# Fused up-sampling attention and token/channel mixer on one core: one list scheduler orders the whole program

## The chip, the cores and the metric

The kernel runs on one core of a Trainium2 chip, as one launch for all eight batches. The metric is the device time of that core in microseconds. Five queues of instructions run beside each other: TensorE (PE, with its weight loads shown apart as PEld), VectorE (DVE), ScalarE (ACT), GpSimd (POOL) and SyncE (SP). Each works its own queue strictly in order; a row that waits holds all rows behind it. DMAs are issued from these queues, here mostly from SP and some from ACT.

## The reference, cut to what matters

```python
q_d, k_d, v_d = (t.reshape(B, H, S // 4, 4, D).mean(axis=3) for t in (q, k, v))
out_up = repeat(softmax(q_d @ k_d.T / sqrt(D)) @ v_d, 4, axis=2)
out_local = softmax(where(abs(pos_i - pos_j) < 4, q @ k.T / sqrt(D), -1e9)) @ v
x = (out_up + out_local), heads side by side      # (B, S, H*D)
h = maximum(x.T @ w_tok1, 0) @ w_tok2
u = x + h.T
out = u + maximum(u @ w_ch1, 0) @ w_ch2
```

There are B = 8 batches, H = 8 heads, S = 576 positions and D = 64; d_model is 512, the hidden sizes are 256 (tokens) and 1536 (channels). All is float32.

## The kernel before

A float32 matrix product is made of three float16 passes (`mm3`, line 124): each operand is split in an upper half and a rest, and the upper halves, and each upper half with the other's rest, are multiplied. So each operand costs an ACT instruction (the upper half) and a DVE instruction (the rest).

A batch `b` passes through these pieces; each is a Python generator that yields `step(engine, us, needs, take, give)` (line 150) before it emits an instruction or a group.

- `load_v` (455) loads eight tiles `vr` of values from SP (`fetch`, 461), squares each on ACT into `dump`, whose accumulator gives `vm` (486), and adds rows pairwise on POOL into `vd` (492, 493). From batch 2 on the tiles carry the tag `w`.
- `pool_q` (506), `pooled` (535) and `local` (592) are the two attentions: scores `sd`, exponentials `pd`, transposes `td` and `ptd`, product `ad` and result `od` for the pooled one; `pooled` ends with ACT issuing the copies of `od` into `vw` (587). The local one has windows of 38 columns, transposes `pT` and `pt`, and the product `av`, from which `x` comes.
- `mix` (666) is the token product: `splits` (675) of `x`, `products` (688) into `t`, `hid` and `t2`, `takes` (715) for `u` and its maximum `umx`, then `scaled` (748) for batches 0 and 1, which makes `uh`, or `mixtures` (766) for later batches. That one makes the four mixtures `s1`, `s2`, `s4`, `s3` of the quarters `a11` to `a22` of `u` on POOL (776), scales all seven to float16 upper halves on ACT (787) and takes their rests on DVE.
- The channel product of batches 0 and 1 is `first` (857, PE rows `c1`, `c<-uh,CW` in the profile) with `first_up` (877). Batches 2 to 7 use `product7` (887): for each of six pairs `p` of weight tiles seven block products with 288 columns instead of eight, in the PSUM banks `P`, `R` and `Q`. ACT copies three of them out (910: `x1`, `m5`, `u2`), DVE adds (955 and others), ACT takes four relus into `h` (918), DVE the rests.
- The block products need sums of weights. `weight_sums` (985) computes them once, on DVE and POOL during batch 1, and stores them in `sums`; `product7` loads three at a time as `t123`.
- `second` (1014, PE rows `c2`, `c<-h,CX` in the profile) and `second_up` (1029) make the second channel product, add it to `u` and store `out` (1039) from SP.

What sets the order: inside `tc.manual_schedule()` the function `drive` (170) is a list scheduler. It holds a clock for each engine in estimated microseconds, and among the next steps of all streams whose needs are made it takes the one that can start first; those of one engine within `PATIENCE` (0.15) of it compete by their rank in the table `ORDER`. In this kernel `drive` orders batch 0 and the beginning of batch 1, until the last `over` of batch 0 and `uh` of batch 1 are made, and returns the streams that are left over.

The rest is driven by hand: a `Run` (1121) steps the channel products of batch `b` in turn with their followers, and `tick` (1142) advances the side work, the attention and the token product of batch `b + 1` (`side`, 846), in proportion to the matmuls issued; `SIDE` = 42 and `FR` = 0.9 are the proportions, and `together` (806) steps up to `LIVE` + 1 streams of it by turns. Outside `manual_schedule` the framework orders instructions itself by priority; `tc.high_priority` and `tc.keep_in_program_order` steer that.

Buffers of the tags `w`, `m`, `g` and `gg` are chosen by `slot` (66). Under `drive`, a step that takes a slot (`take`) sets the number; otherwise `slot` counts up itself:

```python
    def slot(k):

        if not driven[0]:
            now_in[k] = (now_in[k] + 1) % SLOTS[k]
        return k + str(now_in[k])
```

The steps of `load_v` take no slot, and the loads of batch 2 stand within the part that `drive` orders.

Of the kernel before, what the change touches and what calls it, by code (L numbers as in the profile page):

```python
# [6 lines left out]
F32 = mybir.dt.float32  # L7
# [20 lines left out]
FR = 0.9  # L28
LIVE = 3
# [4 lines left out]
ORDER = ("T0 D1 A0 A7 D9 m0 D8 W2 W4 U0 M0 a7 N3 D10 M1 C2 M3 m1 M2 U1 W1 A6 A4 C11 W0 N1 A3 L2 D11 W3 A1 P0 "  # L34
         "C3 m3 D7 A8 S0 m2 H0 P1 C4 C0 L0 D5 D0 D4 a8 A5 L5 L1 h0 a0 Q0 L3 D3 C1 L4 a2 a6 C5 W6 N2 C6 D6 U2 "
         "C10 W7 C9 C8 a1 D2 N0 C7 W5 A2 a3 a4 W8 a5 ").split()
# [7 lines left out]
def tile_ups_attention_mixer(ctx, tc, qk, vw, vr, w1, w2, c1, c2, out):  # L44
# [125 lines left out]
    def drive(streams, until):  # L170

        items = [[g, next(g, None), 0.0, -ORDER.index(name)] for name, g in streams]
        driven[0] = True
        while not all(u in made for u in until):
            some = []
            for it in items:
                if it[1] is None or not may(it[1]):
# [23 lines left out]
            it[2] = t + us + 0.3  # L201
# [3 lines left out]
            try:  # L205
                it[1] = it[0].send(it[2])
            except StopIteration:
                it[1] = None
        driven[0] = False
        for k, n in SLOTS.items():  # L210
            first = min(free[k], key=free[k].get) if free[k] else [i for (x, _), v in held.items() for i in v if x.split(">")[0] == k][0]
            now_in[k] = (first - 1) % n
        return [it for it in items if it[1] is not None]

# [240 lines left out]
    def load_v(st):  # L455
# [18 lines left out]
        early = {0: 8, 1: 5}.get(st.b, 2)  # L474
        for i in range(early):
            yield step("S", ISSUE, *([("mixed", 0)] if st.b == 1 and i == 0 else []))
            fetch(i)
        for i in range(8):
# [3 lines left out]
            if st.b > 1 and i + 2 < 8:  # L482
                fetch(i + 2)
            t = ts.pop(i)
            e = yield step("A", 0.7, at=arrives[i])
            square = nc.scalar.activation(dump, t.rearrange("p r c -> p (r c)"), AF.Square, scale=2.0 ** -20,  # L486
                                          accum_out=st.vm[:, i:i + 1])
            if st.b > 1 and not driven[0]:
                tc.keep_in_program_order(square)
            make(("vm", st.b, i), e)  # L490
            e = yield step("G", 1.25)
# [43 lines left out]
    def pooled(st, pr):  # L535
# [41 lines left out]
        e = yield step("V", 0.65, give=one)  # L577
# [88 lines left out]
    def mix(st):  # L666
# [48 lines left out]
        def takes():  # L715
# [12 lines left out]
            for ch, two in WALK[b > 1]:  # L728
                s0, N = CHUNKS[ch]
                for c in (2 * two, 2 * two + 1):  # L730
                    yield step("A", 0.4, ("t2", b, ch, c), give=f"gg>{b}" if c % 2 else "")
                    if ch == 0:
                        st.u[c] = T([128, S], F32, "ts" if b == 1 and c > 1 else "u", f"u{b}_{c}")
# [491 lines left out]
```

## Time and profile before

| | us |
|---|---|
| runs, median (lowest to highest of three) | 954.78 (953.64 to 956.38) |
| the profiled execution | 949.53 |
| its span, first to last instruction | 947.8 |
| PE busy | 887.2 |
| PE weight loads busy | 659.0 |
| DVE busy | 529.5 |
| ACT busy | 423.6 |
| POOL busy | 297.2 |

The second part of the page cuts the span in 40 slices of 23.7 us; a digit is the busy share in tenths, 9 for 90% and more, and for `PEclk` the granted clock of TensorE in tenths.

```profile
PE   7787899996999989999999999999998999999998
ACT  4764673424432365344643355344653355332620
POOL 5998740412039730064005320054004230002000
PEclk9879999997999999999999999999999999999999
```

Two places show a granted clock under 9: slices 3 and 4 in the start, where weights are prepared, and slice 10, the passage from batch 0 to batch 1. Where a row of the trace has square brackets, they hold the time for which the engine stood idle ahead of it, and what ended that.

### The profile page before, as it was taken

Reading aid. Unit: us, or ns where it says so; the run is one execution under the profiler, and the core shown is the slowest. Engines: PE = TensorE matmul, PEld = TensorE weight load, DVE = VectorE, ACT = ScalarE, POOL = GpSimd, SP = SyncE. Lnnn points to the kernel's source line nnn. Section 1 sums busy time; section 2 is a strip of 40 time slices with the busy share of each in tenths; the row PEclk is TensorE's granted clock in tenths of the full one; section 3 lists DMA queues with packets and bytes.
Section 4 is the critical chain, followed back from the end, with each engine's and each line's share of the span. In section 5 each row is a group of like instructions: output and inputs, shape, how many; then the busy total and the mean of one; then the engine's idle time right before and its main releaser. Section 6 shows DMA issues by size and latency. Waiting matters only on the chain.

```text
span 947.8 us, 26409 instructions
## 1 busy us (share of the span) xinstructions
PE 887.2 (94%) x11218; PEld 659.0 (70%) x11218; DVE 529.5 (56%) x1287; ACT 423.6 (45%) x1004; POOL 297.2 (31%) x457
## 2 busy tenths in 40 slices
PE   7787899996999989999999999999998999999998
PEld 3544678664866758767776778767785768767776
DVE  7888877323667567534755267524754267433631
ACT  4764673424432365344643355344653355332620
POOL 5998740412039730064005320054004230002000
PEclk9879999997999999999999999999999999999999
DMA  9694330511034322340125102350126111100200
GB/s 262 185 297 132 117 81 26 180 34 39 21 136 104 107 64 71 103 157 28 55 90 180 47 30 71 121 140 32 53 89 181 42 35 52 54 21 19 74 20 33
DMA packets 35142, 84.87 MB, mean 90 GB/s; under 512 B 4272, under 2 KB 15536, under 8 KB 33776
## 3 DMA queue, kind: packets, MB, share of 16 engines
q1 hardware_dynamic: 32464, 80.82, 27.9%
q10 hardware_dynamic: 2560, 2.36, 0.9%
q8 instruction: 88, 1.44, 0.6%
q14 instruction: 30, 0.25, 0.1%
HBM read 69.01 MB, written 11.80 MB: 85 GB/s over the span
## 4 chain that ended last, share of the span: by engine, by line
PE 75%; DVE 14%; DMA 4%; ACT 3%; issue 3%; POOL 1%; ACTq 0%; POOLq 0%; DVEq 0%
PE c L124 31%; PE t L124 10%; PE P L124 9%; PE R L124 5%; PE ad L572 3%; PE av L641 3%; PE Q L124 2%; DMA vr<-in_vr_dram 2%; PE t L707 2%; PE sc L605 2%; PE pT L628 2%; PE td L563 2%; DMA vw<-od 1%; PE busy L168 1%; PE sd L544 1%
## 5 line engine op out<-in xcount | busy, mean ns | idle before, releaser
L124 PE MATMUL c<-h,CX 128*128 128x320 f16 (+1 forms) x2304 | 307.3, 286 | 1.3 <-issue 1.3
L124 PEld LDWEIGHTS <-CX 128*128 128x128 f16 x2304 | 222.2, 98 | 66.8 <-issue 5.3
L124 PEld LDWEIGHTS <-CW 128*128 128x128 f16 x1440 | 137.2, 99 | 52.3 <-issue 16.1
L1038 DVE SCALAR_TENSOR_TENSOR u<-c,io,u 128x256 f32<-128x256 f32 (+1 forms) x64 | 32.8, 513 | 103.8 <-PE c L124 103.6
L124 PE MATMUL c<-uh,CW 128*128 128x256 f16 (+1 forms) x576 | 80.7, 293 | 7.2 <-ACT uh L760 6.1
L518 POOL TENSOR_TENSOR qs<-qk 128x288 f32<-128x288 f32 x56 | 43.9, 784 | 137.8 <-DMA qk<-in_qk_dram 134.2
L492 POOL TENSOR_TENSOR vr<-vr 72x256 f32<-72x256 f32 x64 | 47.7, 745 | 113.2 <-ACT dump L486 112.5
L736 DVE TENSOR_REDUCE umx<-u 128x1 f32<-128x256 f32 (+1 forms) x64 | 28.3, 451 | 96.2 <-ACT u L734 96.1
L734 ACT ACTIVATE u<-t,down 128x256 f32<-128x256 f32 (+1 forms) x64 | 30.9, 495 | 102.9 <-PE t L124 102.9
L124 PEld LDWEIGHTS <-t 128*128 128x128 f16 x648 | 61.8, 98 | 18.6 <-issue 2.8
L124 PE MATMUL t<-xh,W 128*128 128x512 f16 (+1 forms) x240 | 61.2, 391 | 4.4 <-DVE xh L685 3.2
L124 PE MATMUL t<-W,hid 128*128 128x256 f16 (+1 forms) x384 | 58.8, 289 | 0.1
L458 POOL MEMSET vd<- 72x16 f32 x8 | 1.0, 123 | 161.9 <-PE ad L572 161.9
L685 DVE SCALAR_TENSOR_TENSOR xh<-x,back,xh 128x512 f16<-128x512 f32 (+1 forms) x40 | 34.0, 849 | 29.3 <-ACT xh L683 29.3
L486 ACT ACTIVATE dump<-vr 72x512 uint8<-72x512 f32 x64 | 39.7, 620 | 15.6 <-DMA vr<-in_vr_dram 15.5
L776 POOL TENSOR_TENSOR s<-u,u 128x288 f32<-128x288 f32 x12 | 9.3, 794 | 115.9 <-ACT u L734 115.9
L572 PE MATMUL ad<-vd,ptd 72*72 72x65 f32 x512 | 40.7, 232 | 3.8 <-issue 2.3
L556 ACT ACTIVATE pd<-sd,nmd 72x144 f32<-72x144 f32 x128 | 39.4, 373 | 9.8 <-DVE nmd L551 8.6
L124 PEld LDWEIGHTS <-W 128*128 128x128 f16 (+1 forms) x240 | 22.6, 99 | 29.4 <-issue 9.8
L572 PEld LDWEIGHTS ad<-vd,ptd 72*72 72x72 f32 x512 | 38.8, 149 | 5.9 <-issue 3.1
L641 PE MATMUL av<-vw,pt 47*32 47x64 f32 x2304 | 36.0, 234 | 6.4 <-issue 3.4
L124 PEld LDWEIGHTS <-hid 128*128 128x128 f16 x384 | 35.1, 98 | 9.5 <-ACT hid L721 0.4
(182 smaller groups left out, 1609.4 us busy)
## 6 DMA issues: line engine op xcount, KB each, us to landing
qk<-in_qk_dram SPq DMA_DIRECT2D x32, 579.0 KB
t<-sums SPq DMA_DIRECT2D x36, 384.0 KB
vw<-in_vw_dram SPq DMA_DIRECT2D x32, 351.0 KB
vr<-in_vr_dram SPq DMA_DIRECT2D x64, 144.0 KB
C_raw<-in_c_dram SPq DMA_DIRECT2D x16, 512.0 KB
out_dram<-u SPq DMA_DIRECT2D x32, 160.0 KB
C_raws<-in_c_dram SPq DMA_DIRECT2D x8, 512.0 KB
out_dram<-u SPq DMA_DIRECT2D x32, 128.0 KB
```

What stands on the lines that cost most here:

```text
L124: nc.tensor.matmul(ps, lhs(a), rhs(c), start=first and i == 0, stop=last and i == 2, **kw)
L486: square = nc.scalar.activation(dump, t.rearrange("p r c -> p (r c)"), AF.Square, scale=2.0 ** -20, accum_out=st.vm[:, i:i + 1])
L492: nc.gpsimd.tensor_add(t[:, 0:2], t[:, 0:2], t[:, 2:4])
L518: nc.gpsimd.tensor_add(two, x[:, :, 0:2], x[:, :, 2:4])
L556: nc.scalar.activation(pd[:, par, g], s[:, par, g], AF.Exp, bias=nm[:, par, g:g + 1], scale=0.125 / 16)
L563: nc.tensor.transpose(ps[:G, par, o:o + G], pd[:, par, g, G * kg:G * kg + G], ident[:G, :G])
L572: nc.tensor.matmul(ps[:, g, par], pt[:, par, kg, G * g:G * g + G], st.vd[:, kg, 2 * pr + par], start=kg == 0, stop=kg == 1)
L641: nc.tensor.matmul(ps[QB * j:QB * j + QB, par, D * hp:D * hp + D], pt[p, hp, QB * j:QB * j + QB], st.vw[h][p, g, D * hp:D * hp + D], start ...
L685: nc.vector.scalar_tensor_tensor(st.xh[t][:, 1], xf(t), back[:n], st.xh[t][:, 0], ALU.mult, ALU.subtract)
L734: nc.scalar.activation(st.u[c][:, s0:s0 + N], banks[ch, c // 2][:, c % 2, :N], AF.Copy, scale=st.down)
L736: nc.vector.tensor_reduce(st.umx[:, ch, c:c + 1], st.u[c][:, s0:s0 + N], axis=AX.X, op=ALU.max, apply_absolute_value=True)
L1038: nc.vector.scalar_tensor_tensor(u, banks[c, ch], io[:, ch:ch + 1], u, ALU.mult, ALU.add)
```

## The change

`drive` takes no `until` any more and runs until every stream has ended; it orders all eight batches inside `manual_schedule`, and `Run`, `tick`, `rest`, `together`, `attention`, `side`, `SIDE` as a number, `FR` and `LIVE` are gone. Every piece of the later batches is a stream with a rank in `ORDER`, and the dependences that were program order become `needs`.

The arithmetic stays. DVE, ACT and POOL have as many instructions as before (1290, 975 and 463 in the order listings); PE has four more matmuls of the filling `busy`, and SP six more stores of weight sums (18 instead of 12).

The scheduler, with the table of ranks:

```diff
-FR = 0.9
-LIVE = 3
...
+SIDE = "h b4 b5 b6 b7 b8 b0 b1 b2 b3 b9 n0 n2 n1 n3 n4 n5"
+SLACK = 0.8
...
+ORDER = ("u0 u1 u2".split() + [f"e{b}.{i}" for b in range(2, 8) for i in (0, 1, 2, 3, 4, 6, 5)] + ORDER
+         + [x[0] + str(b) + "." + x[1:] if x[1:] else x + str(b) for b in range(2, 8) for x in SIDE.split()]
+         + "p0 p1 p2".split() + [f"e{b}.7" for b in range(2, 8)])
...
-    def drive(streams, until):
-
-        items = [[g, next(g, None), 0.0, -ORDER.index(name)] for name, g in streams]
+    def drive(streams):
...
-        while not all(u in made for u in until):
+        while items:
...
-                t = max([clock[e], it[2] if at is None else at] + [made[n] for n in needs]
-                        + [min(free[k.split('>')[0]].values()) for k in take])
+                steady = ("uh", 1, 0) in made
+                t = max([0.0 if steady and at is None and it[4] == e else it[2] if at is None else at]
+                        + [made[n] for n in needs] + [min(free[k.split('>')[0]].values()) for k in take])
+                t = max(clock[e], t + (SLACK if e == "P" and steady else 0.0))
```

So a step of a stream whose last step was on the same engine needs no longer wait for its estimated end once `uh` of batch 1 is made, and a PE step is estimated to start 0.8 us after its last need.

The loads of `vr` take a slot of the tag `w` now, and give it back after the additions on POOL:

```diff
+        held_w = "w>v" if st.b > 1 else ""
         for i in range(early):
-            yield step("S", ISSUE, *([("mixed", 0)] if st.b == 1 and i == 0 else []))
+            yield step("S", ISSUE, *([("mixed", 0)] if st.b == 1 and i == 0 else []), take=held_w)
...
             if st.b > 1 and i + 2 < 8:
+                yield step("S", ISSUE, take=held_w)
...
-            e = yield step("G", 1.25)
+            e = yield step("G", 1.25, give=held_w)
```

`product7` is split in six streams: `copies`, `adds`, `relus`, `rests`, `fetch` (the loads of `t123`) and `products`; every step that used to be in one line of code has a need of its own. The first block product `s1` of a batch needs the whole of `c2` of the batch before, the first `a11` doesn't. Of the new functions the two on which the path runs:

```diff
+        def copies():
+            before = {("x1", 0): ("uh", b, "s2"), ("m5", 0): ("uh", b, "s2"), ("u2", 0): ("uh", b, "s4"),
+                      ("x1", 1): ("uh", b, "s4"), ("m5", 1): ("uh", b, "s3"), ("u2", 1): ("uh", b, "s3")}
+            for p in range(NP):
+                for n, x, r in (("x1", "a11", "P"), ("m5", "s1", "R"), ("u2", "s2", "P")):
+                    e = yield step("A", 0.4, ("p7", b, p, x), before[n, p] if p < 2 else ("rest", b, p - 2, n))
+                    plain[p, n] = T([128, HS], F32, "tm", f"{n}_{b}_{p}")
+                    nc.scalar.copy(plain[p, n], bank[p, r][:, :HS])
+                    make(("plain", b, p, n), e)
...
+                for x, w, r, first, last, needs in (
+                        ("a11", old(fa, 0), "P", True, False, None),
+                        ("s1", new(p, 0), "R", True, False, [("t123", b, p)]),
+                        ("s2", new(p, 1), "P", False, False, [("plain", b, p, "x1")]),
+                        ("a12", old(fa, 1), "Q", True, True, []),
+                        ("s4", old(fb, 1), "R", False, True, [("plain", b, p, "m5")]),
+                        ("s3", new(p, 2), "P", False, False, [("plain", b, p, "u2")]),
+                        ("a11", old(fa + 2, 0), "P", True, False, []),
+                        ("a22", old(fb, 0), "P", False, True, [("add", b, p, "m5")])):
...
+                    if x == "s1":
+                        needs += [("c2", b - 1)]
+                    e = yield step("P", us, ("uh", b, x), *needs, take=f"m>{r}{b}" if first else "")
+                    if first:
```

`mix` has six streams for batches from 2 on: `mixtures` (POOL), `upper` (the conversions on ACT) and `lower` (DVE) stand apart. `t2` of batch `b` needs the output of batch `b - 2` to be over, the final `od` of a batch needs the block products' inputs `("full", b - 1)`, and the local product `av` needs `("mixed", b - 1)`. Buffers of `u` in batch 1 are swapped: tiles 0 and 1 lie in the tag `ts`, which `t123` uses later, instead of 2 and 3. `weight_sums` is two streams, the additions on DVE and `weight_parts` (splits on POOL, three stores for each pair).

```diff
+        for b in range(2, B):
+            streams.append((f"h{b}", lazily(lambda b=b: ahead(b), *after(b - 1))))
+            some = attend(b) + [lazily(lambda b=b: value_scale(ready[b]), *(("vm", b, i) for i in range(8)))]
+            streams += [(f"b{b}.{i}", x) for i, x in enumerate(some)]
+            streams += [(f"n{b}.{i}", lazily(lambda b=b, i=i: mix_of(b)[i], ("q", b, 0))) for i in range(6)]
+            streams += [(f"e{b}.{i}", lazily(lambda b=b, i=i: channel_of(b, i), ("q", b, 3))) for i in range(8)]
+        drive(streams)
```

Three places show how rows move. The first is SP's queue at the end of batch 0 and the beginning of batch 1, with the semaphores for which each row waits: the loads of `vr` of batch 2 (`vr2_i`) and a store of `u0`. Before:

```order
L471 DMA vr2_0_2967<-in_vr_dram 72x512 [waits DMAHW7_49,Activation_49]
L1039 DMA out_0_dram<-u0_2_1284 128x320 [waits DMAHW0_49,DVE_49]
L471 DMA vr2_1_2983<-in_vr_dram 72x512 [waits DMAHW1_49,DMAHW7_49,Activation_49,Pool_49]
L471 DMA vr2_2_2985<-in_vr_dram 72x512 [waits DMAHW1_49,DMAHW2_49,Activation_49,Pool_49]
L471 DMA vr2_3_3023<-in_vr_dram 72x512 [waits DMAHW2_49,DMAHW3_49,Activation_49,Pool_49]
L471 DMA vr2_4_3044<-in_vr_dram 72x512 [waits DMAHW3_49,DMAHW4_49,Activation_49,Pool_49]
```

and in the change:

```order
L471 DMA vr2_0_2967<-in_vr_dram 72x512 [waits DMAHW7_49,Activation_49]
L471 DMA vr2_1_2970<-in_vr_dram 72x512 [waits DMAHW0_49,Activation_49]
L1025 DMA out_0_dram<-u0_2_1282 128x320 [waits DMAHW1_49,DVE_49]
L471 DMA vr2_2_2983<-in_vr_dram 72x512 [waits DMAHW2_49,Activation_49]
L471 DMA vr2_3_3026<-in_vr_dram 72x512 [waits DMAHW3_49,DMAHW7_49,Activation_49,Pool_49]
L471 DMA vr2_4_3057<-in_vr_dram 72x512 [waits DMAHW0_49,DMAHW4_49,Activation_49,Pool_49]
```

Before, every load from the second on waits for POOL, and for the transfer ahead of it; in the change the first three wait for no POOL row, and `vr2_3` is the first that does.

The second place is ACT's queue at the head of batch 3: `u3_c` are the tiles of `u`, `dump` the squares of the `vr` tiles of batch 4, `L619`, `pd4` and `ptd4` attention of batch 4, `a11h3` the first operand of batch 3's block products. Before:

```order
L734 ACTIVATE u3_2_6272<-t2_3_0_2_6174,down3_4959 128x256
L486 ACTIVATE dump_128,vm4_5965<-vr4_7_6172 72x512
L734 ACTIVATE u3_3_6278<-t2_3_0_2_6174,down3_4959 128x256
L734 ACTIVATE u3_2_6272<-t2_3_1_2_6209,down3_4959 128x320
L734 ACTIVATE u3_3_6278<-t2_3_1_2_6209,down3_4959 128x320
L787 ACTIVATE a11h3_6314<-u3_0_6092,us3_0_6298 128x288
```

and in the change:

```order
L734 ACTIVATE u3_3_6173<-t2_3_0_2_6042,down3_5486 128x256
L488 ACTIVATE dump_128,vm4_6059<-vr4_1_6102 72x512
L734 ACTIVATE u3_2_6089<-t2_3_1_2_6163,down3_5486 128x320
L734 ACTIVATE u3_3_6173<-t2_3_1_2_6163,down3_5486 128x320
L488 ACTIVATE dump_128,vm4_6059<-vr4_2_6118 72x512
L619 ACTIVATE P2_112<-P2_112 128x8x38
L488 ACTIVATE dump_128,vm4_6059<-vr4_3_6175 72x512
L619 ACTIVATE P0_110<-P0_110 128x8x38
L619 ACTIVATE P1_111<-P1_111 128x8x38
L566 COPY ptd4_0_6404<-td4_0_6373 72x576
L488 ACTIVATE dump_128,vm4_6059<-vr4_4_6238 72x512
L799 ACTIVATE a11h3_6458<-u3_0_6016,us3_0_6413 128x288
```

One square stood among the last four takes of `u` before; now four stand there and ahead of `a11h3`, with four rows of attention, and a fifth, that of `vr4_0`, in the row just ahead of these.

The third is ACT's queue at the fifth pair of block products of batch 3: `x13`, `m53` and `u23` (in the change `x1_3`, `m5_3`, `u2_3`) are the copies out of PSUM, `h3_4` the relus, and the DMAs from `od4` to `vw4` those of the pooled result of batch 4. Before:

```order
L918 ACTIVATE h3_4_6858<-u23_4_6899 128x288
L587 DMA vw4_0_5884<-od4_6544 8x9x256
L910 COPY x13_4_6944<-P_3_4_6937 128x288
L910 COPY m53_5_6971<-R_3_5_6964 128x288
L918 ACTIVATE h3_4_6858<-m53_4_6866 128x288
L918 ACTIVATE h3_4_6858<-P_3_3_6829 128x288
L632 COPY pt4_0_6963<-pT4_0_6958 128x512
L910 COPY u23_5_6980<-P_3_4_6937 128x288
L587 DMA vw4_0_5884<-od4_6544 8x9x256
```

and in the change:

```order
L922 COPY u2_3_4_7060<-P_3_4_7001 128x288
L587 DMA vw4_0_5886<-od4_6709 8x9x256 x2
L587 DMA vw4_1_5889<-od4_6709 8x9x256 x2
L940 ACTIVATE h3_4_7032<-x1_3_4_7017 128x288
L940 ACTIVATE h3_4_7032<-u2_3_4_7060 128x288
L940 ACTIVATE h3_4_7032<-m5_3_4_7048 128x288
L922 COPY x1_3_5_7105<-P_3_5_7095 128x288
L940 ACTIVATE h3_4_7032<-P_3_4_7001 128x288
L922 COPY m5_3_5_7130<-R_3_5_7114 128x288
```

Before, the first two of the four DMAs stood apart with six rows between them, and the other two later; now all four stand in one row (two rows of x2), ahead of the next relus and copies.

On PE the head of a batch changes too. Before, `second` of a batch ended, and then `a11`, two rows of `sd`, `s1` and `s2` of the next came, six matmuls for each block product. In the change the `a11` of batch 3 (6 matmuls) is followed by 36 matmuls of `c2` of batch 2, and only then by `s1`; `sd4_0` stands in the middle of `second` of batch 2.

More of the change, by code (lines that the diff above doesn't have):

```diff
@@ L207, in drive @@
             except StopIteration:
-                it[1] = None
+                items.remove(it)
         driven[0] = False
[L210 to L213, printed above, removed]
     count = [0]
@@ L764, in scaled @@
                 make(("uh", b, ch), e)
[L766 to L779 removed]
+        ORDER7 = ("a11", "s1", "s2", "a12", "s4", "s3", "a22")
@@ L801, in mixtures @@
-            yield from block("a22", A[1][1])
-            make(("uh", b), now[0])
-        return [splits(), products(), takes(), mixtures() if b > 1 else scaled()]
-    def together(todo, most):
-        live = []
-        while todo or live:
-            while todo and len(live) < most:
-                g = todo.pop(0)
-                live.append([g, next(g)])
-            some = False
-            for x in list(live):
-                if may(x[1]):
-                    some = True
-                    yield x[1]
-                    x[1] = next(x[0], None)
-                    if x[1] is None:
-                        live.remove(x)
-            if not some:
-                yield live[0][1]
@@ L824, in attention @@
-    def attention(st):
-        todo = [pooled(st, pr) for pr in range(4)] + [local(st, t) for t in range(len(TILES))]
-        yield from together([value_scale(st)] + todo, LIVE + 1)
+            make(("uh", b), now[0])
+        return [splits(), products(), takes()] + ([mixtures(), upper(), lower()] if b > 1 else [scaled()])
     def pool_all(st):
@@ L981, in product7 @@
-        make(("h", b), now[0])
-    sums = []
+                    make(("rest", b, p, n), e)
+                make(("hp", b, p), e)
+            make(("h", b), e)
+        return [copies(), adds(), relus(), rests(), fetch(), products()]
+    sums, parts7 = [], {}
     def weight_sums():
-        gates = [("c1", 1, 1, 3), ("c1", 1, 1, 7), ("c1", 1, 1, 11), ("c2", 1, 0, 0), ("c2", 1, 1, 0), ("c2", 1, 0, 1)]
         for p in range(NF // 2):
@@ L1067, in attend, with after @@
                 + [lazily(lambda t=t: local(ready[b], t), ok) for t in range(len(TILES))])
+    def after(b):
+        return [("x", b, t) for t in range(len(TILES))] + [("od", b, i) for i in range(4)]
     mixes = {}
@@ L1103, in tile_ups_attention_mixer @@
         group["Q"] = products[2:]
-        group["h"] = [lazily(lambda: ahead(2), ("x", 1, last))]
-        streams = [(f"{k}{i}", x) for k in "LMCTWUDSANmPHaQh" for i, x in enumerate(group[k])]
-        left = drive(streams, [("over", 0, 3)] + [("uh", 1, 0)] * (B > 1))
-    def rest(items):
-        while items:
-            some = False
-            for it in list(items):
-                if it[1] is None:
-                    items.remove(it)
-                elif may(it[1]):
-                    some = True
-                    yield it[1]
-                    it[1] = next(it[0], None)
-            if items and not some:
-                yield items[0][1]
@@ L1175, in tile_ups_attention_mixer, with late, channel_of @@
-    while work.next is not None:
-        work.go()
+        group["p"], group["u"], group["s"] = [], [], [lazily(f, ("c1", 1, 1, 1)) for f in (weight_sums, weight_parts)]
+        def late(what):
+            yield step("S", 0.0, ("q", 1, 3))
+            if not group["p"]:
+                group["u"], group["p"] = main(ready[1], (["h"] * 4, ["h"] * 4))
+            yield from what()
+        channel = {}
+        def channel_of(b, i):
+            if b not in channel:
+                st, banks = ready[b], {}
+                channel[b] = product7(st) + [second_up(st, banks), second(st, banks)]
+            return channel[b][i]
```

314 lines of the change are left out of this document (123 added, 191 removed).

## The prediction

> **What bounds the kernel now.** I read the head of the page first, to see which engine sets the time.
>
> ```profile
> span 947.8 us, 26409 instructions
> PE 887.2 (94%) x11218; PEld 659.0 (70%) x11218; DVE 529.5 (56%) x1287; ACT 423.6 (45%) x1004; POOL 297.2 (31%) x457
> ```
>
> TensorE is busy for 94% of the span and no other engine for more than 56%, so a reordering can win little more than the 60 us in which PE stands still, and what the throttle takes. Both programs hold the same arithmetic. The next view therefore asks where PE stands: the busy time by stretch, cut at the start of each stage (start and filling; products of batch 0; the passage to batch 1; batch 1; one stretch per batch 2 to 6, from its first block product to that of the next; batch 7). Columns: stretch, length, busy time and count of each engine, granted PE clock, DMA.
>
> ```profile
> core 0: us, PE busy (x) PEld busy (x) DVE busy (x) ACT busy (x) POOL busy (x), PEclk, DMA share, GB/s
> 0.00:102.20 102.20, 78.08 (x1020) 46.53 (x1020) 85.32 (x181) 60.83 (x128) 83.30 (x109) 0.87 0.70 213
> 102.20:205.00 102.80, 101.56 (x1369) 78.36 (x1368) 63.12 (x151) 50.93 (x113) 33.40 (x53) 1.00 0.30 88
> 205.00:240.00 35.00, 25.18 (x178) 17.35 (x177) 12.69 (x36) 14.28 (x41) 9.54 (x16) 0.80 0.12 35
> 240.00:342.10 102.10, 97.22 (x1299) 73.01 (x1297) 63.60 (x149) 33.64 (x79) 54.62 (x91) 1.00 0.31 96
> 342.10:447.75 105.65, 104.08 (x1353) 77.93 (x1353) 55.73 (x142) 50.56 (x125) 27.47 (x47) 0.98 0.27 84
> 447.75:554.07 106.32, 102.62 (x1366) 77.98 (x1364) 55.20 (x143) 48.91 (x122) 26.58 (x45) 1.00 0.27 85
> 554.07:661.76 107.69, 104.03 (x1378) 78.68 (x1375) 57.40 (x148) 51.43 (x128) 29.00 (x47) 1.00 0.28 84
> 661.76:769.82 108.06, 103.95 (x1361) 78.52 (x1362) 53.84 (x141) 47.59 (x118) 24.76 (x44) 0.98 0.28 84
> 769.82:875.87 106.05, 103.52 (x1370) 78.15 (x1368) 55.26 (x143) 45.01 (x108) 6.79 (x9) 1.00 0.12 38
> 875.87:947.80 71.93, 67.01 (x542) 52.52 (x539) 27.35 (x62) 20.39 (x51) 1.71 (x2) 1.00 0.13 42
> ```
>
> Length minus PE busy is PE's idle time: 24.1 us in the start, where DVE and POOL are busy over 80% of the time, 1.2 in batch 0, 9.8 in the passage, 4.9 in batch 1, then 1.6, 3.7, 3.7, 4.1 and 2.5 in the five middle stretches (15.6 together), and 4.9 in the last. The passage is the one sick place: 35 us of which PE works 25.2, at 0.80 of its clock, so at most 20.1 us of work; 14.9 us are lost. The timeline of the passage says why (start, length, engine, line, operation, in brackets the idle time before it and its releaser).
>
> ```profile
> 205.98 27.84 SPq L471 DMA_DIRECT2D vr<-in_vr_dram  x7
> 212.95 0.63 ACT L486 ACTIVATE dump<-vr 72x512 uint8<-72x512 f32 x1 [1.91 <-DMA vr<-in_vr_dram]
> 213.49 0.19 ACT L486 ACTIVATION_READ_ACCUMULATOR dump<-vr 72x1 f32 x1
> 214.60 0.51 POOL L493 TENSOR_TENSOR vd<-vr 72x128 f32<-72x128 f32 x1
> 217.55 0.63 ACT L486 ACTIVATE dump<-vr 72x512 uint8<-72x512 f32 x1 [3.47 <-DMA vr<-in_vr_dram]
> 218.17 0.51 ACT L734 ACTIVATE u<-t,down 128x320 f32<-128x320 f32 x1
> 226.83 0.63 ACT L486 ACTIVATE dump<-vr 72x512 uint8<-72x512 f32 x1 [1.29 <-DMA vr<-in_vr_dram]
> 227.46 0.49 ACT L760 ACTIVATE uh<-u,us 128x256 f16<-128x256 f32 x1
> 228.01 0.59 PE L124 MATMUL c<-uh,CW 128*128 128x256 f16 x2 [3.98 <-ACT uh L760]
> ```
>
> Seven loads of `vr` go out over 27.8 us, one every 4.6 us (212.95 to 217.55): each waits until the tile before it has been squared on ACT and added on POOL. The squares stand in ACT's row ahead of `u` and `uh` of batch 1, so ACT waits for the load, and PE waits 3.98 us for `uh`. The loads go one at a time because all of them sit in one buffer.
>
> **The change, part by part.** (A) The passage. The order listing of SP shows the loads in three buffers: only the fourth waits for POOL. The same loop of 4.6 us then delivers a tile every 1.5 us, and the five that are left after the first three take 7.7 us, beside products that PE has anyway. Of 14.9 us lost I take 13.5 as won. Bounds: 8, if ACT still waits for two of them, and 14.9.
>
> (B) Batch 1, 240 to 342 us: `t2` of batch 2, its maximum and the mixtures of `u` stood at the end, behind the last product; now 132 matmuls of `c2` of batch 1 and first scores of batch 3 stand between the last `t2` and the first block product, and weight sums are done by a stream of their own. POOL is busy 54.6 of these 102 us, so it has room. Idle is 4.9; I take 3.5, between 0 and 4.9.
>
> (C) The heads of batches 2 to 6. Where PE waits there, before:
>
> ```profile
> 454.15 0.77 PE L124 MATMUL P<-a11h,CW 128*128 128x288 f16 x5 [0.74 <-DVE x L955]
> 455.69 0.69 PE L563 MATMUL td<-ident,pd 72*72 72x72 f32 x8 [0.77 <-ACT pd L556]
> 661.76 0.91 PE L124 MATMUL P<-a11h,CW 128*128 128x288 f16 x6 [1.12 <-ACT s4h L787]
> 727.80 0.61 PE L641 MATMUL av<-vw,pt 47*32 47x64 f32 x13 [3.10 <-issue]
> 878.41 0.90 PE L124 MATMUL R<-s1h,t 128*128 128x288 f16 x6 [1.52 <-DVE u L1038]
> ```
>
> The change puts 36 matmuls of `c2` between the first block product and the second, and the first scores of the next batch ahead of both. So the conversions `a11h` to `a22h` have cover, and exponentials are done long before `td` asks. All idle time of the five stretches is 15.6 us; two of them ran at a clock of 0.98, which is another 2% of 105.65 and of 108.06, 4.3 us. Of these 19.9 us I take three quarters, 15: a few waits are left wherever small matmuls follow each other. Bounds: 3 (new waits nearly fill the old ones) and 19.9.
>
> (D) Batch 7: the wait of 1.52 us and a little behind it go, 2 of 4.9; the end is as it was. Bounds 0 and 4.9.
>
> (E) A new wait. The four copies of the pooled result into `vw` are issued from ACT. Before, they stood apart; now they stand in one row of four, ahead of ACT's next copies out of PSUM.
>
> ```profile
> 483.61 1.20 PE L572 MATMUL ad<-vd,ptd 72*72 72x65 f32 x16
> 485.61 0.42 DVE L580 TENSOR_TENSOR od<-ad,rd 72x256 f32<-72x256 f32 x1
> 486.06 0.70 ACTq L587 DMA_DIRECT2D vw<-od  x1
> 486.87 0.40 ACT L910 COPY x<-P 128x288 f32<-128x288 f32 x1 [2.06 <-DVE m L966]
> ...
> 572.02 0.90 PE L124 MATMUL R<-s1h,t 128*128 128x288 f16 x6
> 572.75 0.90 PE L124 MATMUL P<-s2h,t 128*128 128x288 f16 x6
> ...
> L918 ACT ACTIVATE h<-x 128x288 f16<-128x288 f32 x36 | 15.9, 443 | 37.6 <-DVE x L955 37.6
> ```
>
> One issue holds ACT for 0.70 us, and the copy behind it started only at its end (486.76, 486.87). In batch 3 of the change ACT has, from the end of `ad` (484.81 here): 1.25 us to the first issue, 4 x 0.70, three relus of 0.44, the copy `x1` of 0.40: 5.8 us. PE has six block products until it needs that copy, 0.73 us from start to start: 4.4 us. The difference, 1.4 us, is a stall; the other batches stand alike. Five such places, for batches 3 to 7: 7 us lost. Bounds: 0, if ACT or PE runs late there anyway, and 5 x 2.8 = 14.
>
> (F) At nothing: six more stores of weight sums on SP. SP issues a transfer in about 0.4 us (7 loads hold 27.84 us only because they wait), so 2.4 us of a queue that has over 50 us before the sums are read; without that cover they would cost those 2.4 us once. The swap of the buffers of `u` in batch 1 lets the first weight sums be loaded earlier, behind the output of `u` 0 and 1 instead of 2 and 3. The start is reordered a little and gets four more filling matmuls: 0, between -3 and +3, since DVE and POOL bound it and their work is the same.
>
> The sum: -13.5 - 3.5 - 15 - 2 + 7 = -27 us. The profiled execution took 949.53 us in all, 1.7 more than its span, so this gives 922.5 for it. The runs shown have a median of 954.78, 5.25 us above the profiled one; with the same 27 us off the median comes to **928 us**.
>
> The clock deserves a second look, since (E) adds idle time. The passage had 9.8 us of idle and lost 0.20 of 35 us, 7 us, to the clock: if the clock fell in proportion to idle time, 7 us of new waits would cost 5 more, and the sum would be -22. The Trainium skill, "TensorE: Matmul & The Clock Gate", Part 1, says otherwise: the clock halves only when PE has idled through a whole window of about 3.4 us, however many short gaps there are. By that rule the 1.4 us waits cost nothing beyond themselves. The trace agrees: the stretch from 447.75 idles 3.7 us in short pieces at a clock of 1.00, and the passage holds a gap of 3.98. I keep -27.
>
> **The rivals.**
>
> (1) Nothing is left of the gain. ACT is the engine in doubt: a pair of block products needs three copies and four relus on it, 3.0 us of the 5.2 that PE takes, besides attention and squares, and its row is now fixed by estimates. Were 0.7 us lost in each of 36 pairs, 25 us, the time would be 953. For it: (E). Against: ACT is busy 48.9 of 106.3 us in a middle stretch.
>
> (2) Slower. In batches 3 to 6 the change puts five squares of the next batch's `vr` ahead of `a11h` in ACT's row; before, one did. If their loads are late, as in the passage, ACT holds `a11h` and PE stands. Two late tiles of 4.6 us in each of five batches are 46 us: 954.8 - 27 + 46 = 974. It decides as soon as a load lands later than the maximum of `u` is known, since from there the cover is only 36 matmuls of 0.14 us, 5 us. For it: SP's queue is in order, and output stores that wait for DVE stand among these loads. Against: the first three tiles have buffers of their own, and stand in SP's row well before PE's last product of the batch ahead.
>
> (3) The change doesn't do what it says at the passage: buffers are free only on paper, held by exponentials of attention, and the loads still go one by one. Then (A) is 0: 941.
>
> (4) All of it comes off: 14.9 + 4.9 + 19.9 + 4.9 = 44.6, and (E) is hidden: 910. For it: PE's busy records overlap (0.90 us long, 0.73 from start to start), so some idle time is hidden in them. The Trainium skill, "Perfetto Trace Analysis", Identifying the Most-Contended Engine, calls matmul busy time a bad measure for that reason, and looks at the weight loads instead. By that rule the room is 30% of the span, not 6%, and even 910 would be no floor; the trace agrees that busy time overstates, and no run here shows how much a reordering reaches of it.
>
> **How the numbers follow.** My forecast, 913 to 943, has a chance of 0.65; (1) 0.08, (2) 0.08, (3) 0.09, (4) 0.10. The range is 907 to 950: it leaves out (2), half of (1) and a part of (4). Its lower end is 3 us under (4), for what busy records hide; its upper end is the sum with (A) at 8 and (C) at 3 and a little of (E), close to no gain at all. A measurement of this kernel can tell about 0.3%, 3 us, from no change. Faster: 0.65 + 0.09 + 0.10 + a third of (1) = 0.87; same 0.05, the rest of (1); slower 0.08.
>
> **What would show it.** (A): in the changed profile the loads of the first `vr` after batch 0 come in threes, PE's idle time before `c<-uh` of batch 1 is under 2 us, and no slice after the start shows a clock below 0.9. (C): no wait of over 0.5 us for `a11h` to `a22h`. (E): `P<-s2h` or `R<-s4h` waits for an ACT copy once per batch, 1 to 1.5 us, behind four issues in a row. I am wrong if ACT squares wait for DMA ahead of `a11h` (2), if the passage still takes over 30 us (3), or if the middle stretches keep their 106 us although the waits above are gone: then what binds there is not in the order at all.

## The result, and the profile after

The changed kernel takes **921.73 us** (four runs, 919.70 to 926.69), the kernel before in the same comparison 954.21. The ratio is 0.9669, with an interval from 0.962 to 0.9719: 3.3% faster. The profiled execution took 920.09 us with a span of 918.3, so against 949.53 it gained 29.4 us, and by the medians 32.5; the forecast had 27.

Two cuts divide a run of either kernel: the first `c<-uh` of batch 0, and the first product with `s1h` of batch 2. Ahead of the first lies the start, between them batch 0, the passage and batch 1, behind the second the steady part with the heads of batches 3 to 7 (the head of a batch is where its token product ends and its block products begin). The second stretch and the third of the kernel before (columns as in the table by stretch above):

```profile
102.20:343.52 241.32, 225.00 (x2844) 169.21 (x2843) 140.79 (x341) 100.27 (x234) 97.82 (x159) 0.97 0.28 83
343.52:947.80 604.28, 584.15 (x7358) 443.28 (x7356) 303.39 (x768) 262.46 (x644) 116.05 (x190) 1.00 0.23 71
```

and all three of the changed one:

```profile
0.00:104.44 104.44, 79.44 (x1018) 47.92 (x1026) 86.93 (x190) 62.83 (x134) 83.90 (x111) 0.87 0.74 223
104.44:327.24 222.80, 221.25 (x3044) 170.05 (x3043) 150.12 (x352) 102.62 (x239) 96.13 (x152) 0.99 0.28 82
327.24:918.30 591.06, 574.10 (x7156) 441.29 (x7153) 310.36 (x746) 260.54 (x632) 117.96 (x196) 1.00 0.24 73
```

The start lost 2.2 us, the second stretch won 18.5 and the steady part 13.2. About 2 us belong to another line: the change does 192 matmuls `sc` of the local attention earlier, ahead of the second cut (128 of them hold PE for 1.46 us). In the second stretch PE idled 16.3 us before, now 1.6. In the steady part it idled 20.1 us before and 17.0 now; so only 3.2 of the 13.2 us are idle time, and 10.1 are busy time (584.2 to 574.1).

The passage, in the timeline of the changed kernel:

```profile
196.22 0.79 SPq L471 DMA_DIRECT2D vr<-in_vr_dram  x2
202.86 9.55 SPq L471 DMA_DIRECT2D vr<-in_vr_dram  x4
214.33 3.54 SPq L471 DMA_DIRECT2D vr<-in_vr_dram  x2
217.94 0.27 PE L657 MATMUL um_t<-ident,um_m 128*1 128x128 f32 x1 [0.90 <-DVE um_m L654]
218.05 1.54 PE L127 MATMUL c<-uh,CW 128*128 128x256 f16 x12
```

Eight loads go out in 21.7 us, the first two within 0.79, where seven took 27.84 before; `c<-uh` waits for nothing. The signs that the prediction named for (A) came, but for one: the loads go out by two, four and two, not by threes. The longest waits of PE in the steady part are few (what waits and for whom; total, times, longest):

```profile
PE R L127 <- ACT m L922: 3.5, 3, 1.3
PE um_t L657 <- DVE um_m L654: 3.2, 2, 2.2
PE um_t L657 <- ACT P L619: 2.9, 1, 2.9
PE P L127 <- ACT x L922: 1.7, 2, 0.8
PE um_b L663 <- DVE um_m L660: 1.2, 2, 0.9
```

Two kinds make up 12.5 us, most of PE's 17.0 us of idle time there. The waits for the copies `m` and `x` are five, one for each batch, 5.2 us in all: the wait (E) of the prediction. ACT's timeline at one of them:

```profile
566.84 2.88 ACTq L587 DMA_DIRECT2D vw<-od  x4
569.76 0.44 ACT L940 ACTIVATE h<-x 128x288 f16<-128x288 f32 x1 [4.36 <-DMA vw<-od]
...
570.78 0.38 ACT L922 COPY x<-P 128x288 f32<-128x288 f32 x1
```

Four issues hold ACT for 2.88 us, the copy ends at 571.16, and the product behind it, ready since the end of its forerunner, had waited 0.85 us. The other kind, 7.3 us at the heads of batches 3 to 5, the prediction did not have. The timeline at the longest:

```profile
626.62 1.54 POOL L783 TENSOR_TENSOR s<-u,u 128x288 f32<-128x288 f32 x2
627.17 4.32 DVE L617 TENSOR_TENSOR P<-P,mx 128x304 f32<-128x304 f32 x1
628.12 1.53 POOL L783 TENSOR_TENSOR s<-s,u 128x288 f32<-128x288 f32 x2
...
631.81 0.14 DVE L654 TENSOR_REDUCE um_m<-umx 128x1 f32<-128x8 f32 x1
...
632.10 0.27 PE L657 MATMUL um_t<-ident,um_m 128*1 128x128 f32 x1 [2.90 <-ACT P L619]
```

One subtraction on DVE, 0.47 us elsewhere, lasts 4.32 us, as long as POOL works through its additions for the mixtures. The maximum `um_m` stands behind it, and PE waits 2.90 us for it. (The releaser named, ACT's `P`, ran at the same time; the row that PE needs is `um_m`.) The clock fell behind it, as three stretches of 2 us show:

```profile
630.00:632.00 2.00, 0.00 (x0) 0.00 (x0) 2.00 (x4) 0.46 (x1) 2.00 (x3) 1.00 0.00 0
632.00:634.00 2.00, 1.90 (x44) 1.51 (x45) 1.86 (x5) 0.62 (x2) 0.52 (x2) 0.79 0.23 74
634.00:636.00 2.00, 2.00 (x10) 1.08 (x8) 1.93 (x6) 0.97 (x3) 1.40 (x2) 0.50 0.00 0
```

PE has work again from 632 on, but for some 4 us at 0.79 and 0.50 of its clock. (In e5, the same kernel again, it did not fall there; see the point on the clock below.)

### The profile page after: what moved, and what is told of

It is laid out like the page before. It is cut to its first block, busy times and chain, and to the rows that moved or that the text cites. A ratio compares the mean times of both kernels' runs of the same rounds, so it can differ in the third digit from the quotient of the medians.

```text
span 918.3 us, 26400 instructions
## 1 busy us (share of the span) xinstructions
PE 874.8 (95%) x11215; PEld 659.3 (72%) x11222; DVE 547.4 (60%) x1287; ACT 426.0 (46%) x1004; POOL 298.0 (32%) x457
## 4 chain that ended last, share of the span: by engine, by line
PE 82%; DVE 8%; DMA 3%; ACT 2%; issue 2%; POOL 1%; ACTq 1%; POOLq 0%; DVEq 0%
PE c L127 37%; PE P L127 11%; PE t L127 10%; PE R L127 5%; PE ad L572 3%; PE av L641 3%; PE Q L127 3%; PE t L707 2%; PE sd L544 2%; PE pT L628 2%; DMA W_raw<-in_w_dram 2%; PE sc L605 2%; PE td L563 1%; DVE P L617 1%; ACTq L587 1%
## 5 line engine op out<-in xcount | busy, mean ns | idle before, releaser
L127 PE MATMUL c<-h,CX 128*128 128x320 f16 (+1 forms) x2304 | 301.3, 287 | 0.0
L518 POOL TENSOR_TENSOR qs<-qk 128x288 f32<-128x288 f32 x56 | 38.8, 693 | 244.3 <-DMA qk<-in_qk_dram 240.5
L492 POOL TENSOR_TENSOR vr<-vr 72x256 f32<-72x256 f32 x64 | 51.1, 798 | 124.4 <-ACT dump L488 123.9
L127 PE MATMUL c<-uh,CW 128*128 128x256 f16 (+1 forms) x576 | 77.5, 290 | 0.1
L127 PEld LDWEIGHTS <-t 128*128 128x128 f16 x648 | 62.6, 98 | 18.6 <-issue 2.6
L127 PE MATMUL t<-xh,W 128*128 128x512 f16 (+1 forms) x240 | 59.2, 383 | 2.0 <-DVE xh L685 2.0
L646 ACT ACTIVATE x<-av,up 128x512 f32<-128x512 f32 (+1 forms) x40 | 27.0, 683 | 34.1 <-PE av L641 34.1
L619 ACT ACTIVATE P<-P 128x304 f32<-128x304 f32 (+1 forms) x40 | 18.2, 456 | 51.1 <-DVE P L617 50.9
```

Source lines behind the costliest of these rows:

```text
L127: nc.tensor.matmul(ps, lhs(a), rhs(c), start=first and i == 0, stop=last and i == 2, **kw)
L492: nc.gpsimd.tensor_add(t[:, 0:2], t[:, 0:2], t[:, 2:4])
L518: nc.gpsimd.tensor_add(two, x[:, :, 0:2], x[:, :, 2:4])
L646: nc.scalar.activation(x.rearrange("p hp two d -> p two hp d"), ps[:n, :, :4 * D].rearrange("p two (hp d) -> p two hp d", hp=4), AF.Copy, ...
```

## The experiments

All times are medians; the ratio is to the kernel before, and "second" and "steady" are the lengths of the two stretches in the profiled run.

| kernel | us | ratio (interval) | second | steady |
|---|---|---|---|---|
| before | 953.3 to 955.1 | 1 | 241.3 | 604.3 |
| the change, again (e5) | 922.49 | 0.9665 (0.9633 to 0.9697) | 222.8 | 589.4 |
| e1 before, `vr` in several buffers | 947.97 | 0.9945 (0.9914 to 0.9975) | 236.6 | 609.4 |
| e2 change, `vr` of batch 2 in one | 938.96 | 0.9834 (0.9808 to 0.9861) | 238.8 | 589.6 |
| e3 change, all copies into `vw` on SP | 931.27 | 0.9745 (0.9712 to 0.9777) | 228.6 | 593.0 |
| e4 change, mixtures on DVE | 916.05 | 0.9607 (0.9572 to 0.9642) | 223.7 | 581.4 |
| e6 change, `vw` of batches 2 to 7 on SP | 928.28 | 0.9734 (0.9702 to 0.9766) | 225.8 | 592.6 |
| e7 change, `a11` behind `c2` | 922.24 | 0.9659 (0.9626 to 0.9693) | 222.6 | 589.3 |
| e8 change, e4 and e6 together | 913.15 | 0.9564 (0.9529 to 0.9599) | 225.6 | 576.7 |
| e9 as e8, scale of `u` late | 933.13 | 0.9778 (0.9735 to 0.9821) | 226.1 | 599.0 |
| e10 change, `SLACK` 0 | 924.72 | 0.9696 (0.9656 to 0.9735) | 229.3 | 588.6 |
| e11 change, mixtures ordered late | 933.38 | 0.9772 (0.9725 to 0.9818) | 229.2 | 594.1 |

The start took 104.4 to 111.2 us in these runs, and 104.4 and 106.4 in two profiles of the change itself, so single profiles are compared by the other two stretches. The profile of the kernel before is 5 us faster than its median and that of e1 5 us slower than its own, so the steady parts of these two, 604.3 and 609.4, can't be compared; the other profiles lie within 4 us of their medians.

> The change itself once more, beside the next three on the same chip. All theories: 919 to 926, and the stretch from the first s1 product of batch 2 to the end lasts 589 to 592 us.

This came as expected; the change has 0.9669 and 0.9665 in two comparisons.

**e1: the buffers alone, in the kernel before.**

```diff
+        held_w = "w>v" if st.b > 1 else ""
...
+                yield step("S", ISSUE, take=held_w)
                 fetch(i + 2)
...
-            e = yield step("G", 1.25)
+            e = yield step("G", 1.25, give=held_w)
```

> The kernel before, with one thing of the change: the loads of vr take a slot of the tag w and give it back after the additions, so they go through several buffers. Theory 1 (the single buffer made the passage sick): the 18.4 us between the first and the second matmul group of c<-uh of batch 1 shrink to 4 to 8 us, the granted clock there stays over 0.9, and the time falls by 8 to 14 us to 940 to 946; the rest of the 24 us that the change won between batch 0 and batch 2 stays lost. Rival (only the new order of the streams cures the passage, since ACT still takes the squares ahead of uh): less than 4 us.

Between the two: 5 us by the ratio, 7 by the medians. The waits for `uh` went, but the last load went out only at 220.51, and the wait moved (timeline of e1):

```profile
224.03 0.63 ACT L488 ACTIVATE dump<-vr 72x512 uint8<-72x512 f32 x1 [2.78 <-DMA vr<-in_vr_dram]
...
225.00 0.28 PE L659 MATMUL vm_t<-ident,vm_m 72*1 72x72 f32 x1 [2.55 <-DVE vm_m L656]
```

PE's order of before has `vm_t` of batch 2, which needs all eight squares, at this place. PE waits 2.55 us for it, and the clock is at 0.50 from 226 to 234.

**e2: the change without them.** The eight tiles of batch 2 take one slot and give it back after the last.

```diff
-                ts[i] = T([G, 4, 128], F32, tag, f"vr{st.b}_{i}")
+                if st.b == 2:
+                    ts["tag"] = ts.get("tag") or slot("w")
+                    ts[i] = sb.tile([G, 4, 128], F32, tag=ts["tag"], name=f"vr{st.b}_{i}", bufs=1)
```

> The change, but the eight vr tiles of batch 2 share one buffer as before. Theory 1: the loads come one every 4.6 us again, ACT's squares hold u and uh of batch 1, PE waits at the passage, and the time rises by 10 to 18 us to 932 to 940. Rival (the new order has enough c2 matmuls of batch 0 at this place to cover the loads): under 4 us, 921 to 925.

As theory 1 has it: 17 us slower than the change, 16 of them in the second stretch. In the timeline of e2:

```profile
214.19 13.99 SPq L475 DMA_DIRECT2D vr<-in_vr_dram  x4
...
227.66 0.37 PE L661 MATMUL um_t<-ident,um_m 128*1 128x128 f32 x1 [2.67 <-DVE um_m L658]
...
241.33 1.24 PE L548 MATMUL sd<-qd 64*72 64x144 f32 x8 [6.46 <-POOL vr L496]
```

One tile in 4.6 us, and PE waits where rows assumed the tiles done. The new order without the buffers is worth 955.1 - 939.0 = 16 us, the buffers without the new order 5 to 7, both 32. At the passage each alone does little: the second stretch falls by 2.5 us with the order alone (e2), by 4.7 with the buffers alone (e1), and by 18.5 with both.

**e3 and e6: the copies into `vw` from SP.** In e6 for batches 2 to 7, in e3 for all. The edit of e6, with lines cut at `...`:

```diff
-            e = yield step("A", 2.9 if b < 2 else 0.2, ("vw", b), *(("od", b, i) for i in range(3)), at=e)
+            e = yield step("A" if b < 2 else "S", 2.9 if b < 2 else 4 * ISSUE, ("vw", b), *(("od", b, i) for i in range(3)), at=e)
...
-                    nc.scalar.dma_start(...
+                    (nc.scalar if b < 2 else nc.sync).dma_start(...
```

> The change, but the four copies of od into vw are issued from SP and no longer from ACT. Theory 2 (the row of four issues on ACT makes the waits for the copies x1 and m5): the five waits R<-s4h and P<-s2h for ACT, 5.2 us together, go, and the time falls by 4 to 6 us to 916 to 918. Rival (ACT is late there by its other rows): the waits stay, and the time stays within 2 us.

> As the change with the copies into vw on SP, but for batches 2 to 7 only, so that batches 0 and 1 keep ACT's. Theory 2 (the four issues in a row on ACT cost a wait at each head): the waits of PE for the ACT copies x1 and m5, 5.2 us in the change, fall under 1.5; the stretch from the first s1 of batch 2 to the end falls by 4 to 6 us against the change, and the time with it, to 915 to 920. Rival (what ACT loses there is hidden or comes back as a wait of av for the copies, which now stand behind loads of t123 on SP): within 2 us of the change, with waits of av for DMA.

Both missed: slower by 9 and 6 us. e3 also moved rows of batches 0 and 1 (waits of `av` for the copies at 164 to 171 us), which is why e6 left these alone. The waits of PE in e6, from 327 to 850 us:

```profile
PE um_t L657 <- ACT P L619: 11.7, 4, 2.9
PE P L127 <- DVE m L929: 0.8, 1, 0.8
```

The waits for ACT's `x` and `m` are gone, as theory 2 has it. But the list scheduler, with other estimates, put other rows together, and four heads now have a DVE row of 4.32 us (in the change two have one, and a third one of 3.71), each with a wait of 2.9 and a clock of 0.97 to 0.98 over its stretch. PE's idle time in the steady part is as in e5, 16.7 us against 17.0; its busy time rose from 572.4 to 575.9, with four falls of the clock where e5 has none. The rival's wait of `av` came only to 0.2 us in e6. So e6 doesn't measure what it was meant to; e8 does.

**e4: the mixtures on DVE.**

```diff
-                    e = yield step("G", 0.85, *all_u, ...
+                    e = yield step("V", 0.45, *all_u, ...
...
-                    nc.gpsimd.tensor_tensor(t[i], blocks()[x][i], blocks()[y][i], op)
+                    nc.vector.tensor_tensor(t[i], blocks()[x][i], blocks()[y][i], op)
```

> The change, but the eight additions for the mixtures of u of each batch from 2 on stand on DVE instead of POOL (3.6 us more of DVE at each head). Theory 3 (a run of six of them on POOL holds up a DVE instruction, which lasts 4.3 instead of 0.5 us, and with it the maximum of u): no DVE instruction of over 2 us is left in batches 2 to 6, the waits of um_t and um_b of 7.1 us fall under 2, and the time falls by 3 to 7 us to 915 to 919. Rival (DVE is late at the heads because it has too much to do there): the waits grow by 3 us for each of six heads, and the time rises by 5 to 20 us.

As theory 3 has it, and against its rival: DVE has more to do and PE waits less. The steady part fell by 8.1 us against e5 (under 1 us of it are 68 matmuls that stand ahead of the cut now). The DVE group of this subtraction from 327 to 850 us, first of the change, then of e4 (count, busy time, mean ns of one, idle before):

```profile
L617 DVE TENSOR_TENSOR P<-P,mx 128x304 f32<-128x304 f32 (+1 forms) x22 | 19.0, 863 | 0.8
```

```profile
L617 DVE TENSOR_TENSOR P<-P,mx 128x304 f32<-128x304 f32 (+1 forms) x22 | 12.0, 546 | 0.8
```

The mean falls from 863 to 546 ns. What is left of PE's waits in e4:

```profile
PE P L127 <- ACT x L922: 4.3, 5, 0.9
PE um_t L657 <- DVE um_m L654: 1.3, 4, 0.3
```

**e11: the mixtures on POOL, but later in the order.** Their steps need the scale of `u` in the scheduler; nothing on POOL waits for it.

```diff
-                    e = yield step("G", 0.85, *all_u, ... *([("uh", b, "s1")] if name == "s3" else []))
+                    e = yield step("G", 0.85, *all_u, ... *([("uh", b, "s1")] if name == "s3" else []), ("us", b))
...
+            make(("us", b), now[0] + 0.5)
```

> The change, but the mixtures, still on POOL, start only behind the scale of u. Theory 3 (a DVE instruction with two inputs in SBUF stands still while POOL works off a row of additions): the waits of um_t go, but now the rests of a11h or s1h, or an attention row, on DVE last 1.5 to 4.5 us, and PE waits for them at the heads, since the cover behind a11 is 5 us; the time stays within 6 us of the change, 917 to 928. Rival (the long DVE rows came from the maximum's own place, not from POOL): no DVE row of over 1.5 us, and the time falls by 5 us or more.

Slower by 11 us, beyond both. The long row is there again, at three heads, and at two of them it moved one step down the chain (timeline of e11):

```profile
431.48 5.25 DVE L617 TENSOR_TENSOR P<-P,mx 128x304 f32<-128x304 f32 x1
431.87 1.54 POOL L783 TENSOR_TENSOR s<-u,u 128x288 f32<-128x288 f32 x2
...
434.87 1.54 POOL L783 TENSOR_TENSOR s<-u,s 128x288 f32<-128x288 f32 x2
...
436.99 0.58 PE L663 MATMUL um_b<-um_m,ones 1*128 1x1 f32 x2 [4.24 <-DVE um_m L660]
```

The mechanism held and its price was too low: the wait is 4.24 us, and 4.09 at the head of batch 5, where the row falls between the two halves of the maximum. The third long row, 4.69 us at 325 us, stands at the head of batch 2, where PE waits 2.48 us for a transpose `pT`; this is part of the 6.4 us that the second stretch is longer than in e5. The clock of the stretches with these waits is 0.97 to 0.99.

**e8: both edits.**

> The change with the mixtures on DVE and the copies into vw of batches 2 to 7 on SP. Theories 2 and 3 together: what each gave adds up; idle time of PE from the first s1 of batch 2 to the end, 17 us in the change, falls to 4 to 8, and the time is 4 to 6 us under that of the change with the mixtures on DVE alone, 909 to 913. Rival (both fill the same slack): no better than the mixtures alone, 914 to 918.

Steady 576.7 us against 581.4 of e4, so the copies on SP are worth 4.7 there, or a little over 4, since e8 has 48 matmuls more ahead of the cut. Of these 4.7 PE's idle time gives 2.1 (10.1 to 8.0): the waits for ACT go, and waits for DVE's `m` come in part in their place. By the ratios it is 4 us under e4, by the medians 3 (the intervals overlap), at the lower edge of what was expected; the second stretch took 1.9 us longer. No wait for ACT is left among PE's waits from 327 to 850 us:

```profile
PE P L127 <- DVE m L929: 3.2, 5, 0.7
PE P L127 <- issue: 0.5, 1, 0.5
PE um_t L657 <- DVE um_m L654: 0.3, 1, 0.3
```

e8 beats both kernels: 0.9564.

**e7: nothing between `a11` and `s1`.**

```diff
-                    if x == "s1":
+                    if x == "s1" or x == "a11":
```

> The change, but the first a11 product of a batch needs the whole of c2 of the batch before, as s1 does, so nothing stands between a11 and s1 as a cover. Theory 4 (the 36 matmuls of c2 between them, some 4.9 us, are what hides the conversions a11h to a22h): waits for s1h, s2h and for ACT and DVE rows behind a11 of 2 to 5 us at each of five or six heads, and the time rises by 8 to 25 us to 930 to 947. Rival (other side work fills the place, or the heads were never bound there): within 3 us.

Theory 4 falls: 922.24 us, no difference, though the first `a11` stands 0.7 us ahead of `s1` in e7 and 3.2 to 7.4 in the change. The timeline of e7 at the head of batch 3 says why:

```profile
424.83 0.27 PE L657 MATMUL um_t<-ident,um_m 128*1 128x128 f32 x1 [2.24 <-DVE um_m L654]
...
439.90 0.90 PE L127 MATMUL P<-a11h,CW 128*128 128x288 f16 x6
440.63 0.90 PE L127 MATMUL R<-s1h,t 128*128 128x288 f16 x6
```

The maximum of `u` is taken 15.8 us ahead of `s1`. In the kernel before, the six distances are 4.0 to 7.7 us, in the change 11.7 to 18.2.

**e9: the maximum late again, on e8.**

```diff
-            yield step("V", 0.0, *all_u)
+            yield step("V", 0.0, *all_u, ("c2", b - 1, 0, 3))
```

> The kernel of e8 (mixtures on DVE, copies into vw on SP), but the maximum of u, from which all conversions come, waits for the last but one group of c2 of the batch before, so that about 36 matmuls of c2, 4.9 us, are left between it and s1, as in the kernel before (there um_t stood 4 to 8 us ahead of s1, in e8 9 to 12). Theory 5 (the heads gain because the token product is done earlier, not because a11 is): waits of 1 to 4 us return at each of five or six heads, and the time rises by 6 to 20 us over e8, to 919 to 933. Rival (the heads gain by the order of rows alone): within 3 us of e8, 911 to 916.

20 us slower than e8, all in the steady part (599.0 against 576.7); the distance is 4.3 to 6.8 us, in e8 8.8 to 11.8. The head of batch 3 in the timeline of e9:

```profile
437.53 0.27 PE L657 MATMUL um_t<-ident,um_m 128*1 128x128 f32 x1
...
445.11 0.95 ACT L799 ACTIVATE s4h<-s,us 128x288 f16<-128x288 f32 x2
445.96 0.38 ACT L922 COPY x<-P 128x288 f32<-128x288 f32 x1
...
446.39 0.77 PE L127 MATMUL P<-s2h,t 128*128 128x288 f16 x5 [1.81 <-ACT x L922]
```

ACT converts five operands in a row, the copy `x` stands behind them, and PE waits 1.81 us. Such waits at the six heads make 8.3 us of the 14.2 by which PE's idle time grew (8.0 to 22.2). So in this order an early maximum of `u`, and with it early conversions, is worth some 20 us. How much of it the heads of the kernel before lost isn't shown: its order was another, and its waits ahead of `a11` and `s1` at the heads add to 4.6 us.

**e10: `SLACK` 0.**

> The change with SLACK 0 in place of 0.8. Theory 6 (the slack keeps PE rows behind their ACT and DVE rows far enough that real durations and latencies do not stall PE): idle time of PE from the first s1 of batch 2 to the end rises from 17 to 30 us or more, and the time rises by 10 to 25 us. Rival (the order is set by needs and ranks, the slack changes little): within 4 us of the change.

Theory 6 falls: 2 us, within the noise, and PE idles 18.6 us in the steady part, not 30. `SLACK` moved waits about (three DVE rows of 3.9 us stand in e10 too) and is worth little.

## Why the prediction was right, and where it was not

The sign and the size came out: 928 forecast, 921.73 measured, inside 913 to 943. The steady part's share of that agreement is luck, as the second point shows. Point by point:

- **(A) and (B), -17.** The second stretch gave -18.5, or -20.7 with the earlier `sc`. The mechanism, loads in one buffer, is shown by e2. The split was wrong: (A) had the buffers win 13.5 us "beside products that PE has anyway". e1 shows that PE has no such products in the old order; `vm_t` takes the place of `uh` as the wait. The gain is of both parts together. Nor did a tile come every 1.5 us: four loads took 9.55, and the order covered them.
- **(C) and (D), -17, with (E), -10.** The steady part gave -13.2, or -11 without the shift of `sc`. The old waits went, as (C) had it: of 20.1 us of idle time some 4.5 are left beside the two new kinds of wait, and `td`, which had waited 2.8 us, waits 0.1. But three errors nearly cancel in the sum. First, the step "the change puts 36 matmuls of `c2` between the first block product and the second", which was to give the cover, is worth nothing (e7); `um_t` stands 12 to 18 us ahead, and e9 shows on e8 what a late one costs. Second, the bound of 19.9 us was made of idle time and clock, but busy time fell by 10.1 us too, and little of this is clock (see below): `c<-h` in the steady part has 1728 matmuls before and 1731 after, at a mean of 286 and 288 ns, and 230.1 against 224.7 us of busy time. In a row of 24 of them (before, at 211 us, 3.42 us long) they start some 0.14 us apart, so a record of 286 ns can hide a pause behind it, and the change has longer rows (about 105 rows of `c<-h` where there were about 150). Rival (4) said so, and the sum didn't use it. Third, a wait was missing: the row on DVE, 8.1 us by e4.
- **(E), +7.** Right in place, order and number of places; 5.2 us of waits, and 3 to 4.7 by e8 against e4. The stall is 0.85 or 1.32 us each, not 1.4.
- **(F), 0.** The start was 2.2 us longer in this profile, within the 3 allowed. But the two profiles with the old order have 102.2 and 104.9 us, and the other ten with the new one 106.3 to 111.2, so a loss of a few us there is likely; it was not tested.
- **Rivals.** (2) didn't come: ACT waits 3.7 us in all for `vr` ahead of its 64 squares, 15.5 before, and none of PE's waits over 0.4 us in the steady part is for `a11h`. ACT's group in the changed kernel (the last column is the idle time before it and its releaser):

```profile
L488 ACT ACTIVATE dump<-vr 72x512 uint8<-72x512 f32 x64 | 39.9, 623 | 4.0 <-DMA vr<-in_vr_dram 3.7
```

  (3) didn't come (e2 shows its price, 17 us, not 13.5). (1) needed ACT to be late 36 times; it is late five times. (4) needed (E) to be hidden; e8, where (E) and the row on DVE are gone, takes 913, near its 910.
- **The clock.** The prediction kept -27 because the page cited there, "TensorE: Matmul & The Clock Gate", Part 1, in the Trainium skill, has the clock halve only after a whole idle window of about 3.4 us, and it found that the trace agrees. It does only in part. In the passage the clock had fallen to 0.50 at 220 us, behind a gap of 2.38 us and ahead of the one of 3.98. At the head of batch 2 it fell behind gaps of at most 0.58 us (the kernel before; the column ahead of the last two is the clock):

```profile
340.00:342.00 2.00, 0.98 (x5) 0.75 (x6) 1.63 (x11) 1.00 (x4) 2.00 (x4) 1.00 0.34 135
342.00:344.00 2.00, 1.52 (x6) 0.80 (x7) 1.94 (x7) 2.00 (x6) 0.57 (x2) 0.55 0.00 0
```

  Nor does the length of one gap decide. Gaps of 1.60 us in e1, at 504 and 729 us, were followed by 0.51 and 0.50; the gap of 2.90 us in the change was followed by 0.50, and one of 2.92 us in e5, the same kernel at the same place, by nothing:

```profile
634.00:636.00 2.00, 1.84 (x47) 1.48 (x48) 1.90 (x6) 0.60 (x3) 0.58 (x2) 1.00 0.23 74
```

  The measurement decides: shorter waits can bring the clock down too. The five waits of 0.85 and 1.32 us did not, so the 5 us that the prediction weighed against its sum did not come. One fall costs little: the one behind 632 us (0.79, 0.50 and 0.86 over three stretches of 2 us) took 1.7 us of clock, and the steady part of the change is 1.6 us longer than that of e5.

By the granted clock, as an estimate, PE lost 2.7 us in the steady part before (0.58 over the 2.5 us from 343.5 on, 0.50 and 0.67 over two stretches of 2 us from 728 on) and 1.7 in the change. So the clock explains about 1 us of the 10.1 by which busy time fell; the earlier `sc` explain about 2 more. What stays open is where the other 7 us come from: pauses inside the records are the likely place, and no run here shows them apart.

## What to carry to other kernels

When a scheduler takes over a whole program, ask first how far ahead of its use each operand is ready, not which row stands between two others: taking the maximum of `u` 4 to 7 us ahead of `s1` instead of 9 to 12 cost 20 us (e9 against e8), and moving the product `a11` next to `s1` cost nothing (e7). A buffer that serialises loads and an order that needs them early may have to be mended together, as here at the passage. And when one edit shifts a list scheduler's estimates, look for a wait that came elsewhere before judging the edit: moving four DMA issues was 6 us slower alone, and faster once the row on DVE was cured.

## What the runs showed of the hardware

A DVE instruction with two operands in SBUF stood still for as long as POOL worked through a run of additions on SBUF: 3.71 and 4.32 us, instead of 0.47, in the change, 4.32 in e6, 3.85 to 3.90 in e10 and up to 5.25 in e11; with the additions on DVE (e4, e8) no DVE row of the steady part exceeds 1.1 us. The Trainium skill, "SBUF — State Buffer", at its single rule, has such a DVE instruction contend with a GpSimd instruction that reads SBUF, for a shared port that one holds for its whole instruction. The traces agree, and go further: the wait outlasted one POOL instruction of 0.77 us and went on over five in a row. So a row of short additions on POOL can block DVE for as long as all of it together. The kernel before had the same additions on POOL, and no DVE row over 1.2 us in its steady part; it was the new order that brought the two together.
